# A list scheduler that knows a shared port, bounds that read their own limits, and a new set of rank offsets

## The chip, the cores and the metric

The kernel runs on one core of one Trainium2 chip. The metric is the device time of one execution in microseconds (us). Before the change the median of three runs is 272.78 us (271.49 to 273.32). The core has five engines that matter here, each with its own instruction queue that runs in order: TensorE (PE) multiplies matrices, VectorE (DVE), ScalarE (ACT) and GpSimd (POOL) do elementwise work, and SyncE (SP) issues most of the transfers (DMAs). PE writes into PSUM, a small memory of eight banks from which DVE and ACT read; POOL works on SBUF, the large on-chip memory.

## The reference

Two layers follow each other. The first is attention over 4 batches and 8 heads, 768 positions of 64 numbers, in which each query sees only 6 of the 24 chunks of 32 keys:

```python
k_chunks = k.reshape(B, H, nc, chunk, D)
k_min = np.min(k_chunks, axis=3)
k_max = np.max(k_chunks, axis=3)
ub = np.sum(np.maximum(q[:, :, :, None, :] * k_min[:, :, None, :, :], q[:, :, :, None, :] * k_max[:, :, None, :, :]), axis=-1)
ub = np.where(causal, ub, -1000000000.0)
top_chunks = np.argsort(ub, axis=-1)[..., -top_k:]
scores = scale * np.matmul(q, k.transpose(0, 1, 3, 2))
mask = sel & (pos[:, None] >= pos[None, :])
scores = np.where(mask, scores, -1000000000.0)
...
attn = attn / (np.sum(attn, axis=-1, keepdims=True) + 1e-09)
return np.matmul(attn, v).astype(np.float32)
```

The second is a dense pair of layers over all 3072 tokens: `h = x @ w_in` (512 to 2048), `g = h * clip(h + 3, 0, 6) / 6`, and `g @ w_out` (2048 to 512).

## The kernel before, in words

**Tiling.** Two heads make a pair (16 pairs in all), and 768 queries are two halves of 384, with 12 chunks each. A *unit* is two pairs in one half; there are 16 units, numbered 0 to 15, four to a batch: units 0 and 1 are half 0 of batch 0, units 2 and 3 its half 1, and so on. A dense *group* is one half of one batch: 384 tokens.

**The steps of a unit.** `prepare` turns K and Q so that the head dimension lies on the partitions: in batch 0 by PE (tiles KT and QT, then copies to KF and QF by ACT or DVE), in the other batches by DVE transpositions (L343). Each half of K of a pair then gives 12 chunk limits: the maximum and the minimum of each chunk (`limits`, two DVE reductions, L356 and L357), and their difference (L359, POOL or DVE). The limits are kept in KMA, 32 columns for maximum less minimum and 32 for the minimum, of which 24 are used: columns 0 to 11 for half 0, 12 to 23 for half 1. Q also gives its relu (QR, L367, ACT). Casts by POOL or DVE (L297, L295) put K and Q in bf16 into KL and QLA.

`bounds` (L389) is the matmul that gives the upper bounds UBT of a unit: for each head, the weights are 32 columns of limits (all of a pair's, whichever half the queries are), the moving operand is QF and then QR. For units 4 and later two units are done in one joint step. `attend` then makes, on DVE, the unit's selection: `bounds_in` transposes UBT to UB (and for half 0 adds BIAS, which takes future chunks away), `largest` finds the eight largest (L404), `select` compares with the sixth (L409), writes a shift (L412) into SELA and transposes SELA to the masks MT (L414). Two `masks_out` steps copy MT into QLA beside the queries (L226, L228 or L230: ACT, DVE or POOL). The scores (SPS, L430) then come out of PE with the masks in them; ACT takes the exponentials (PT, L440), POOL clears the triangle (L445), PE multiplies with V (PVP, L461), and DVE divides and writes Xb (L467, L473).

**The dense part of a group.** XT holds the group's tokens turned (by PE and DVE for the first three groups, by DVE transposition and a way through DRAM, BT, BD, BF, for the other five). For each of 16 blocks of the hidden layer PE makes HP (L518), ACT makes U (L523), DVE makes GT (L526); then PE makes three output tiles OP of 16 matmuls each (L533), which ACT or DVE evict to OT (L559, L561) and SP stores.

**What sets the order.** All of this is recorded as steps of a `Plan`, each with the engines that may do it and a length on each, a rank, the steps it comes after, and the buffers that it takes and gives back. `Plan.order` is a list scheduler: it walks through the time of its own model, and whenever an engine is free it starts the ready step of lowest rank for which there are buffers. A step that may go to several engines goes to the one that the model says ends sooner. The rank of a step is its unit's or group's, plus an offset of the kind (the table RANK), plus an offset of the single step from the table SHIFT, whose keys are the numbers of steps in order of their creation; some -2000 is as much as "as soon as possible", +2000 "as late as possible". The kernel's instructions are written out in the order that this gives, each on its engine's queue. On the chip only queues, semaphores and buffers remain: a wait is set wherever an instruction reads or overwrites something that an earlier one in this order wrote or read, by the memory that the two touch.

Four banks of PSUM (`m`) are shared by KT, QT, UBT, PVP, XTP, HP and OP; two double banks (`s`) hold scores. SP's queue has the loads of K, Q and V as well as the stores, in the planner's order, so a load stands behind a store whose tile is not evicted yet.

## Time and profile before

| | |
|---|---|
| median of three runs | 272.78 us |
| profiled execution, its own time | 272.74 us |
| its span, from the first to the last instruction | 271.0 us |
| PE busy | 257.9 us, 95% |
| DVE busy | 220.3 us, 81% |
| ACT busy | 183.1 us, 68% |
| POOL busy | 138.8 us, 51% |
| mean granted clock of PE | 0.994 |

Busy shares are means over stages with different limits. PE's share counts the time in which a matmul is in flight: one that was started and then waits for an input of the next, or runs at a lower clock, counts too. So the profile is read by stage, and within a stage by the spacing of the instructions and by what each of them waited for. In the timeline's rows the first number is the start in us, the second the length; "x16" says that 16 instructions of the kind are merged; and the brackets at the end hold the engine's idle time before the row, and what ended it. The names of instructions are out<-in by tiles. In the rows of groups of instructions the numbers are total busy us, mean ns of one, and the idle time before them.

### The profile page before, as it was taken

Reading aid. Unit: us, or ns where it says so; the run is one execution under the profiler, and the core shown is the slowest. Engines: PE = TensorE matmul, PEld = TensorE weight load, DVE = VectorE, ACT = ScalarE, POOL = GpSimd, SP = SyncE. Lnnn points to the kernel's source line nnn. Section 1 sums busy time; section 2 is a strip of 40 time slices with the busy share of each in tenths; the row PEclk is TensorE's granted clock in tenths of the full one; section 3 lists DMA queues with packets and bytes.
Section 4 is the critical chain, followed back from the end, with each engine's and each line's share of the span. In section 5 each row is a group of like instructions: output and inputs, shape, how many; then the busy total and the mean of one; then the engine's idle time right before and its main releaser. Section 6 shows DMA issues by size and latency. Waiting matters only on the chain.

```text
span 271.0 us, 6300 instructions
## 1 busy us (share of the span) xinstructions
PE 257.9 (95%) x2244; PEld 151.5 (56%) x2244; DVE 220.3 (81%) x605; ACT 183.1 (68%) x297; POOL 138.8 (51%) x309
## 2 busy tenths in 40 slices
...
GB/s 163 221 214 206 203 186 130 182 125 131 194 123 180 146 173 132 158 160 98 137 142 150 190 177 169 54 0 143 93 2 58 60 77 5 95 97 41 39 39 79
DMA packets 122720, 33.70 MB, mean 124 GB/s; under 512 B 113217, under 2 KB 118081, under 8 KB 122689
## 3 DMA queue, kind: packets, MB, share of 16 engines
...
q8 instruction: 17, 0.28, 0.5%
q14 instruction: 15, 0.11, 0.2%
...
## 4 chain that ended last, share of the span: by engine, by line
PE 56%; DVE 27%; ACT 5%; DMA 4%; SPq 3%; issue 2%; ACTq 1%; DVEq 0%
PE OP L533 19%; PE HP L518 19%; PE SPS L430 9%; PE PVP L461 5%; DVE GT L526 4%; PE UBT L389 3%; SPq L210 3%; DVE KMA L357 3%; DVE KMA L356 2%; DMA QS<-in_q_dram 2%; DVE QLA L228 2%; DVE T L404 2%; ACT PT L440 2%; DVE MT L414 2%; DVE Xb L473 2%
## 5 line engine op out<-in xcount | busy, mean ns | idle before, releaser
L440 ACT ACTIVATE PT<-SPS 128x1024 bf16<-128x1024 f32 (+2 forms) x96 | 86.1, 941 | 27.3 <-PE SPS L430 27.0
L518 PE MATMUL HP<-XT,WIN 128*128 128x384 bf16 x512 | 89.4, 326 | 0.2 <-DVE GT L526 0.2
L533 PE MATMUL OP<-WOUT,GT 128*128 128x512 bf16 x368 | 85.5, 379 | 0.0
L523 ACT ACTIVATE U<-HP,THREE 128x384 bf16<-128x384 f32 x128 | 72.6, 611 | 16.7 <-PE HP L518 13.5
L526 DVE SCALAR_TENSOR_TENSOR GT<-U,HP 128x384 bf16<-128x384 bf16 x128 | 66.3, 546 | 16.3 <-ACT U L523 13.3
L518 PEld LDWEIGHTS <-WIN 128*128 128x128 bf16 x512 | 49.3, 98 | 31.0 <-issue 0.3
L445 POOL TENSOR_SCALAR_AFFINE_SELECT PT<-PT 128x256 bf16<-128x256 bf16 x96 | 39.1, 421 | 46.7 <-ACT PT L440 45.5
L533 PEld LDWEIGHTS <-GT 128*128 128x128 bf16 x368 | 35.0, 98 | 37.9 <-issue 1.4
L430 PE MATMUL SPS<-QLA,KL 128*128 128x384 bf16 (+2 forms) x320 | 49.9, 283 | 4.1 <-DVE QLA L228 1.9
L430 PEld LDWEIGHTS <-KL 128*128 128x128 bf16 x320 | 28.4, 99 | 22.4 <-issue 7.4
L297 POOL TENSOR_SCALAR_AFFINE_SELECT KL<-KF 64x384 bf16<-64x384 f32 x63 | 32.0, 508 | 17.2 <-DVE KF L343 12.7
L297 POOL TENSOR_SCALAR_AFFINE_SELECT QLA<-QF 64x384 bf16<-64x384 f32 x60 | 30.6, 510 | 13.5 <-PE SPS L430 6.4
L461 PEld LDWEIGHTS <-PT 128*128 128x128 bf16 x672 | 24.7, 98 | 5.3 <-POOL PT L445 1.1
L461 PE MATMUL PVP<-VB,PT 128*128 128x65 bf16 x672 | 26.2, 194 | 0.3 <-POOL PT L445 0.3
L367 ACT ACTIVATE QR<-QF 128x384 f32<-128x384 f32 x24 | 12.8, 559 | 12.0 <-DVE QF L343 12.0
L473 DVE TENSOR_TENSOR Xb<-PVP,RINV 128x384 bf16<-128x384 f32 x32 | 18.6, 580 | 1.1
L561 DVE TENSOR_SCALAR OT<-OP 128x512 f32<-128x512 f32 x7 | 4.8, 692 | 17.1 <-PE OP L533 17.1
L511 POOL COPY XT<-BF 128x384 bf16<-128x384 bf16 x20 | 9.9, 534 | 15.9 <-DMA BF<-BD 15.9
L559 ACT ACTIVATE OT<-OP 128x512 f32<-128x512 f32 x16 | 9.5, 596 | 12.1 <-PE OP L533 12.0
L356 DVE TENSOR_REDUCE KMA<-KF 128x12 f32<-128x384 f32 x24 | 13.1, 544 | 1.0 <-PE UBT L389 0.6
L228 DVE COPY QLA<-MT 64x768 bf16<-64x768 bf16 x29 | 13.1, 453 | 0.9
L343 DVE STREAM_TRANSPOSE KF<-KS 128x384 f32<-128x384 f32 x24 | 13.2, 561 | 0.0
...
## 6 DMA issues: line engine op xcount, KB each, us to landing
...
KS<-in_k_dram SPq DMA_DIRECT2D x24, 192.0 KB, 5.1
QS<-in_q_dram SPq DMA_DIRECT2D x24, 192.0 KB, 5.9
VT<-in_v_dram SPq DMA_DIRECT2D x24, 192.0 KB, 4.5
...
```

Source lines behind the costliest of these rows:

```text
L228: nc.vector.tensor_copy(to, x)
L297: nc.gpsimd.affine_select(out=to, in_=x, pattern=[[0, n]], compare_op=A.is_ge, fill=0.0, base=0, channel_multiplier=0)
L356: nc.vector.tensor_reduce(out=over, in_=chunks, axis=X_AXIS, op=A.max)
L430: nc.tensor.matmul(SP[:, j, c0:c0 + n], lhsT=KLS[st["pair"] % 6][:, j, jb * P:(jb + 1) * P], rhs=st["QL", half][:, j, at:at + n], start=Tr ...
L440: nc.scalar.activation(PT[:, :, 0:cols], SP[:, :, 0:cols], ACT.Exp, scale=scale)
L445: nc.gpsimd.affine_select(out=PT[:, :, c0:c0 + P], in_=PT[:, :, c0:c0 + P], pattern=[[0, 2], [1, P]], compare_op=A.is_ge, fill=0.0, base=0 ...
L461: nc.tensor.matmul(PVP[:, j, n, :], lhsT=PT[:, j, c0:c0 + P], rhs=st["VB"][:, jb, j, :], start=(jb == 0), stop=(jb == qb))
L473: nc.vector.tensor_tensor(out=to, in0=PVP[:, :, :, 0:D], in1=RINV[:].to_broadcast([P, 2, HB, D]), op=A.mult)
L518: nc.tensor.matmul(HP[:], lhsT=WIN[:, kt, f * P:(f + 1) * P], rhs=g["XT"][:, kt, :, :], start=(kt == 0), stop=(kt == KT_HID - 1))
L523: nc.scalar.activation(U[:], g["HP", f][:], ACT.Relu, bias=THREE[:], scale=1.0)
L526: nc.vector.scalar_tensor_tensor(out=g["GT"][:, f, :], in0=g["U", f][:], scalar=6.0, in1=g["HP", f][:], op0=A.min, op1=A.mult)
L533: nc.tensor.matmul(g["OP", t][:], lhsT=g["GT"][:, f, t * P:(t + 1) * P], rhs=WOUT[:, f, :], start=(f == 0), stop=(f == FT - 1))
```

## The change

The planner gets two things. A step may be marked `port`, and then the model starts a marked DVE step, or any POOL step, only when the other of these two engines is through with such a step; and each PE step has a kind of tiling (`tiles`: "bounds" or none), and the model adds 0.1 us where it changes. Several model lengths change with this.

The selection of a unit becomes up to five steps instead of three: `bounds_in` (the transposition), `future` (BIAS, half 0 only), `largest`, `select`, and `select_out` (the transposition to MT). SELA has two tiles, one for each half, instead of four, and a selection comes after the `select_out` before it of the same half.

The limits lie in KMA in 13 slots of 44 columns, 20 of zeros and then 24 of limits. The bounds of half 1 take the 24 limits and 8 zeros of the slot behind; those of half 0 take 20 zeros and the 12 limits of half 0. The bounds of half 0 are therefore found in columns 20 to 31 of UB.

Because the numbers of steps change, SHIFT is replaced as a whole; RANK stays. By the orders of the two kernels, no engine's total of instructions changes but for these: five mask copies go from DVE to ACT (DVE 29 to 24, ACT 2 to 7), and a few copies and casts change between DVE, ACT and POOL.

```diff
--- before.py
+++ after.py
@@ -25,17 +25,22 @@
 
 
 SHIFT = {
...
-    2046.3, 1409: 34.8, 1412: -200.2, 1460: 182.7, 1466: 73.7, 1494: 165.9, 1500: 13.6, 1527: 53.8, 1557: -171.6
+    55: 1045, 73: 1112.4, 76: 239.7, 77: 132.9, 79: 237.7, 92: 165.4, 93: 130.6, 100: 149.9, 102: 300.3, 108: 7.6, 122: 76.2, 131: -1918.7, 134: -2103.4,
...
+    -1958.8, 1583: -2045.9
 }
 
 
@@ -52,11 +57,11 @@
         self.room, self.steps = {kind: list(range(n)) for kind, n in room.items()}, []
         self.lane, self.lanes, self.lean = 0, room["lane"], {}
 
-    def add(self, engine, length, rank, run=None, after=(), take=(), give=()):
+    def add(self, engine, length, rank, run=None, after=(), take=(), give=(), port=False, tiles=None):
 
 
         step = dict(lengths=engine if isinstance(engine, dict) else {engine: length}, rank=(rank + SHIFT.get(len(self.steps), 0), len(self.steps)),
-                    run=run, told=isinstance(engine, dict), take=take, give=give, then=[])
+                    run=run, told=isinstance(engine, dict), port=port, tiles=tiles, take=take, give=give, then=[])
         step["wait"] = {e: len(after) for e in step["lengths"]}
         for other in after:
             other["then"].append(step)
@@ -86,6 +91,7 @@
     def order(self, **busy):
 
         free = {e: busy.get(e, 0.0) for e in self.BEHIND}
+        port, tiles = dict(DVE=0.0, POOL=0.0), None
         ready = {e: [] for e in self.BEHIND}
 
         def behind(step, own):
@@ -125,8 +131,15 @@
                         for held in st["take"]:
                             held[2] = self.take(held[0])
                         out.append(st)
-                        st["at"], st["engine"], st["length"] = now, e, st["lengths"][e]
-                        free[e] = now + st["length"]
+                        begin = now
+                        if e == "POOL" or e == "DVE" and st["port"]:
+                            begin = max(now, port["DVE" if e == "POOL" else "POOL"])
+                            port[e] = begin + st["lengths"][e]
+                        if e == "PE":
+                            begin += 0.1 * (st["tiles"] != tiles)
+                            tiles = st["tiles"]
+                        st["at"], st["engine"], st["length"] = begin, e, st["lengths"][e]
+                        free[e] = begin + st["length"]
                         n += 2
                         heapq.heappush(events, (free[e], n, st, True))
                         heapq.heappush(events, (free[e] + self.BEHIND[e], n + 1, st, False))
@@ -165,6 +178,8 @@
     HS = S // 2
     HC = NCH // 2
     scale = 1.0 / np.sqrt(D)
+    OWN = 32 - HC
+    KM = NCH + OWN
 
     const = ctx.enter_context(tc.tile_pool(name="const", bufs=1))
     ps_score = ctx.enter_context(tc.tile_pool(name="ps_score", bufs=1, space=bass.MemoryType.PSUM))
@@ -257,12 +272,12 @@
     nc.gpsimd.memset(BIAS[:], 0.0)
     nc.gpsimd.affine_select(out=BIAS[:], in_=BIAS[:], pattern=[[1, 8], [-1, 8]], compare_op=A.is_ge,
                             fill=-1e9, base=0, channel_multiplier=0)
-    SELA = const.tile([P, 4, HC, 32], BF16, name="SELA")
+    SELA = const.tile([P, 2, HC, 32], BF16, name="SELA")
     nc.gpsimd.memset(SELA[:], 0.0)
     THREE = const.tile([P, 1], FP32, name="THREE")
     nc.vector.memset(THREE[:], 3.0)
-    KMA = const.tile([P, 6, 2, 32], FP32, name="KMA")
-    nc.vector.memset(KMA[:, :, :, HC:32], 0.0)
+    KMA = const.tile([P, 13, KM], FP32, name="KMA")
+    nc.vector.memset(KMA[:, :, 0:KM - NCH], 0.0)
     for r in (0, 96):
         nc.vector.tensor_scalar(EB[r:r + 32, :].rearrange("p (c w) -> p c w", w=CH),
                                 IDENT32[r:r + 32, r:r + NCH].unsqueeze(2).to_broadcast([32, NCH, CH]), -MASK,
@@ -308,8 +323,7 @@
     for i in range(6):
         KLS.append(const.tile([P, 2, S], BF16, name=f"KL{i}"))
     QLS = [QLA[:, i, :, :] for i in range(6)]
-    KMS = [KMA[:, i, :, :] for i in range(6)]
-    SELS = [SELA[:, i, :, :] for i in range(4)]
+    SELS = [SELA[:, i, :, :] for i in range(2)]
     VBS = [const.tile([P, NBLK, 2, D + 1], BF16, name=f"VB{i}") for i in range(6)]
 
     xpool = ctx.enter_context(tc.tile_pool(name="xpool", bufs=1))
@@ -351,7 +365,7 @@
     def limits(st, half, part, e="DVE"):
 
         chunks = st["KS", half][:].rearrange("p (c w) -> p c w", w=CH)
-        over, low = (KMS[st["pair"] % 6][:, which, half * HC:(half + 1) * HC] for which in range(2))
+        over, low = (KMA[:, 2 * (st["pair"] % 6) + which, KM - NCH + half * HC:KM - NCH + (half + 1) * HC] for which in range(2))
         if part == 0:
             nc.vector.tensor_reduce(out=over, in_=chunks, axis=X_AXIS, op=A.max)
             nc.vector.tensor_reduce(out=low, in_=chunks, axis=X_AXIS, op=A.min)
@@ -375,6 +389,11 @@
     def at_column(u, i, j):
 
         return 2 * (j if u["n"] % 2 and u["joint"] else 1 - j) + i
+
+    def chunk_limits(st, half, which):
+
+        c0 = (2 * (st["pair"] % 6) + which) * KM + (KM - NCH) * half
+        return KMA[:].rearrange("p s c -> p (s c)")[:, c0:c0 + 32]
 
     def bounds(us):
         for u in us:
@@ -386,30 +405,35 @@
                     for j in range(2):
                         r = slice(64 * j, 64 * j + 64)
                         g = 32 * at_column(u, i, j)
-                        nc.tensor.matmul(u["UBT"][g:g + 32, :], lhsT=KMS[st["pair"] % 6][r, which, :],
+                        nc.tensor.matmul(u["UBT"][g:g + 32, :], lhsT=chunk_limits(st, u["half"], which)[r, :],
                                          rhs=(st["QR", u["half"]] if which == 0 else st["QS", u["half"], "F"])[r, :], start=(which == 1), stop=(which == 0))
 
     def bounds_in(u):
         UB = u["UB"] = work.tile([P, HC, 32], FP32, name="UB", tag=tag("ub"), bufs=1)
         nc.vector.transpose(UB[:].rearrange("p t c -> p (t c)"), u["UBT"][:])
-        if u["half"] == 0:
-            nc.vector.tensor_tensor(out=UB[:, 0:8, 0:8], in0=UB[:, 0:8, 0:8], in1=BIAS[:], op=A.add)
+
+    def future(u):
+        nc.vector.tensor_tensor(out=u["UB"][:, 0:8, OWN:OWN + 8], in0=u["UB"][:, 0:8, OWN:OWN + 8], in1=BIAS[:], op=A.add)
 
     def largest(u):
         T8, UB, half = small.tile([P, HC, 8], FP32, name="T8", tag="t8"), u["UB"], u["half"]
         u["T8"] = T8
         if half == 0:
-            nc.vector.tensor_reduce(out=T8[:, 0:TOPK, 0], in_=UB[:, 0:TOPK, 0:TOPK], axis=X_AXIS, op=A.max)
+            nc.vector.tensor_reduce(out=T8[:, 0:TOPK, 0], in_=UB[:, 0:TOPK, OWN:OWN + TOPK], axis=X_AXIS, op=A.max)
         for t in range(0 if half else TOPK, HC):
-            nc.vector.max(out=T8[:, t, :], in_=UB[:, t, 0:max(8, half * HC + t + 1)])
+            c0 = 0 if half else OWN
+            nc.vector.max(out=T8[:, t, :], in_=UB[:, t, c0:c0 + max(8, half * HC + t + 1)])
 
     def select(u):
-        SEL, T8, UB, half = SELS[u["n"] % 4], u["T8"], u["UB"], u["half"]
-        at, nch = (slice(0, HC), NCH) if half else (slice(TOPK, HC), HC)
+        SEL, T8, UB, half = SELS[u["half"]], u["T8"], u["UB"], u["half"]
+        at, nch, c0 = (slice(0, HC), NCH, 0) if half else (slice(TOPK, HC), HC, OWN)
         nc.vector.scalar_tensor_tensor(
             out=SEL[:, at, 0:nch], in0=T8[:, at, TOPK - 1:TOPK].to_broadcast([P, at.stop - at.start, nch]), scalar=-5e8,
-            in1=UB[:, at, 0:nch], op0=A.max, op1=A.is_gt)
+            in1=UB[:, at, c0:c0 + nch], op0=A.max, op1=A.is_gt)
         nc.vector.tensor_scalar(SEL[:, :, NCH:NCH + 1], T8[:, :, 0:1], CAP, 0.0, op0=A.subtract, op1=A.max)
+
+    def select_out(u):
+        SEL, half = SELS[u["half"]], u["half"]
         MT = u["MT"] = work.tile([P, HS], BF16, name="MT", tag=tag("mt"), bufs=1)
         nc.vector.transpose(MT[:], SEL[:].rearrange("p t c -> p (t c)"))
 
@@ -650,7 +674,7 @@
     vs = hold("gt", 2 * H // 2, 1)
     for i in range(6):
         late = there["WOUT", 0] if i >= 4 else []
-        made["EB", i] = [add(dict(POOL=0.85) if late else dict(DVE=0.52, ACT=0.81), None, 25 if late else RANK["eb"], later(beside, i, j), after=late)
+        made["EB", i] = [add(dict(POOL=0.85) if late else dict(DVE=0.52, ACT=0.81), None, 25 if late else RANK["eb"], later(beside, i, j), port=True, after=late)
                          for j in range(2)]
         made["ones", i] = add("POOL", 0.17, 25 if late else -3, later(ones, i), after=late)
     n_queries = 0
@@ -694,11 +718,11 @@
                                        after=here + (in_order[-1:] if name == "QS" else []), take=[held[f]], give=used)
 
             a = turned["KS"]
-            made["K", p, half] = [add(castings(first), None, r + lead + 1, later(keys, st, half, j),
+            made["K", p, half] = [add(castings(first), None, r + lead + 1, later(keys, st, half, j), port=True,
                                       after=[a] + free.get(("KL", p - 6), []), give=[held["kf"]]) for j in range(2)]
             b1 = add("DVE", 0.95 if first else 0.93, r + lead, later(limits, st, half, 0), after=(direct["KS"] if first else [a]) + free.get(("KM", p - 6), []),
                      give=[bank_of["KS"] if first else held["kf"]])
-            chain.append(add(dict(POOL=0.17, DVE=0.08) if first else dict(POOL=0.17), None, r + lead, later(limits, st, half, 1), after=[b1]))
+            chain.append(add(dict(POOL=0.17, DVE=0.08) if first else dict(POOL=0.17), None, r + lead, later(limits, st, half, 1), after=[b1], port=True))
 
             st["QL", half] = QLS[n_queries % 6]
             n_queries += 1
@@ -709,7 +733,7 @@
                 u["qf", p][1] = 4
             chain += [c, add(dict(ACT=0.45, DVE=0.5) if first else dict(ACT=0.42), None, r + lead, later(queries, st, half, "relu"), after=direct["QS"] if first else [c],
                              take=[u["qr", p]], give=[bank_of["QS"] if first else u["qf", p]])]
-            made["Q", p, half] = [add(castings(first), None, r + lead + 1, later(queries, st, half, j),
+            made["Q", p, half] = [add(castings(first), None, r + lead + 1, later(queries, st, half, j), port=True,
                                       after=[c] + free.get(("QL", n_queries - 7), []), give=[u["qf", p]]) for j in range(2)]
             st["q", half] = n_queries - 1
 
@@ -718,14 +742,14 @@
             r = 10.0 * us[0]["n"]
             used = [u[name, st["pair"]] for u in us for st in u["two"] for name in ("qf", "qr")]
             held = [hold("m") for u in us]
-            a = add("PE", 1.5 * slow if len(us) == 1 else 1.9, r + RANK["sel"], later(bounds, us), after=sum([u["chain"] for u in us], []),
+            a = add("PE", 1.36 * slow if len(us) == 1 else 1.38, r + RANK["sel"], later(bounds, us), tiles="bounds", after=sum([u["chain"] for u in us], []),
                     take=held, give=used)
             for u, m in zip(us, held):
                 u["bounds"], u["ubt"] = a, m
                 for st in u["two"]:
                     free.setdefault(("KM", st["pair"]), []).append(a)
 
-    held_results = {}
+    held_results, selected = {}, {}
 
     def attend(u):
         nonlocal order_of_scores
@@ -733,12 +757,16 @@
         n, two, half = u["n"], u["two"], u["half"]
         r = 10.0 * n
         ub, mt = hold("ub"), hold("mt", 2)
-        a = add("DVE", 0.94 if half == 0 else 0.61, r + RANK["sel"], later(bounds_in, u), after=[u["bounds"]], take=[ub], give=[u["ubt"]])
-        a = add("DVE", 0.59 if half == 0 else 1.07, r + RANK["sel"], later(largest, u), after=[a])
-        a = add("DVE", 1.07 if half == 0 else 1.25, r + RANK["sel"], later(select, u), after=[a], take=[mt], give=[ub])
+        a = add("DVE", 0.51, r + RANK["sel"], later(bounds_in, u), after=[u["bounds"]], take=[ub], give=[u["ubt"]])
+        if half == 0:
+            a = add("DVE", 0.17, r + RANK["sel"], later(future, u), after=[a], port=True)
+        a = add("DVE", 0.56 if half == 0 else 1.0, r + RANK["sel"], later(largest, u), after=[a])
+        a = add("DVE", 0.29 if half == 0 else 0.52, r + RANK["sel"], later(select, u), after=[a] + selected.get(half, []), give=[ub], port=True)
+        a = add("DVE", 0.55, r + RANK["sel"], later(select_out, u), after=[a], take=[mt])
+        selected[half] = [a]
         mask = []
         for j in range(2):
-            mask.append(add(dict(DVE=0.46, ACT=0.83, POOL=0.9), None, r + RANK["sel"] + j, later(masks_out, u, j),
+            mask.append(add(dict(DVE=0.46, ACT=0.83, POOL=0.9), None, r + RANK["sel"] + j, later(masks_out, u, j), port=True,
                             after=[a] + mask + sum([free.get(("QL", st["q", half] - 6), []) for st in two], []), give=[mt]))
 
         begun = []
@@ -765,7 +793,7 @@
                     if q0 == jb * P:
                         parts.append(add("POOL", 0.37, r + RANK["tri"], later(triangle, st, half, t, c0), after=[e]))
             if st["b"] == 0:
-                parts.append(add(dict(ACT=0.42, DVE=0.35), None, r - 3, later(cast_values, st, half), after=there["V", p, half], give=[vs]))
+                parts.append(add(dict(ACT=0.42, DVE=0.46), None, r - 3, later(cast_values, st, half), after=there["V", p, half], give=[vs], port=True))
                 parts.append(made["ones", p])
                 if half == 1:
                     parts.append(made["V", p])
```

24 rows, old and new, of the table SHIFT are left out of this document.

## The prediction

> **What bounds the kernel now.** First the page's busy shares, then stages cut where TensorE (PE) changes its rate.
>
> ```profile
> PE 257.9 (95%) x2244; PEld 151.5 (56%) x2244; DVE 220.3 (81%) x605; ACT 183.1 (68%) x297; POOL 138.8 (51%) x309
> ```
>
> ```profile
> 0.00:3.75 3.75, 0.00 (x0) 0.03 (x1) 2.75 (x5) 0.79 (x1) 3.00 (x13) 1.00 0.52 116
> 3.75:29.61 25.86, 20.95 (x156) 11.50 (x157) 23.97 (x77) 19.87 (x37) 21.08 (x50) 1.00 1.22 214
> 29.61:36.97 7.36, 7.22 (x65) 4.32 (x65) 6.00 (x15) 4.66 (x6) 3.72 (x9) 0.77 1.18 201
> 36.97:267.40 230.43, 229.72 (x2025) 135.61 (x2023) 186.83 (x509) 157.74 (x255) 111.00 (x242) 1.00 0.66 113
> 267.40:271.00 3.60, 0.00 (x0) 0.00 (x0) 0.76 (x2) 0.00 (x0) 0.00 (x0) 1.00 0.23 75
> ```
>
> Each row gives the length, then busy time of PE, its weight loads, VectorE (DVE), ACT and POOL, then the granted clock. From 36.97 us, where the first dense matmul (HP) stands, PE is busy 229.72 of 230.43 us. Its work is the same in both kernels, so a new order can win only the time that PE spends badly. That lies in two places. Until 29.61 us DVE is busy 23.97 of 25.86 us and PE merely follows it. Later, a few instructions last too long because they hold an input that is not ready. The last 3.60 us (eviction and store) stay as they are.
>
> The second place shows in the timeline, at the joint bounds (UBT) of two units: a clean group first, then two others.
>
> ```profile
> 85.16 1.45 PE UBT L389 x32
> ...
> 76.75 1.50 PE L389 MATMUL UBT<-QF,KMA 64*32 64x384 f32 x12
> 77.04 0.54 DVE L357 TENSOR_REDUCE KMA<-KF 128x12 f32<-128x384 f32 x1
> 77.69 0.15 PEld L389 LDWEIGHTS UBT<-QF,KMA 64*32 64x32 f32 x5 [0.79 <-ACT QR L367]
> 79.15 5.35 PE L533 MATMUL OP<-WOUT,GT 128*128 128x512 bf16 x24
> ...
> 120.86 1.34 PE L389 MATMUL UBT<-QF,KMA 64*32 64x384 f32 x14
> 121.09 0.54 DVE L357 TENSOR_REDUCE KMA<-KF 128x12 f32<-128x384 f32 x1
> 121.69 0.11 PEld L389 LDWEIGHTS UBT<-QF,KMA 64*32 64x32 f32 x2 [0.66 <-DVE KMA L357]
> 123.10 1.25 PE L533 MATMUL OP<-WOUT,GT 128*128 128x512 bf16 x5
> ```
>
> The clean group holds PE for 1.45 us. The one at 76.75 holds it until the next OP at 79.15, 2.40 us; the one at 120.86 until 123.10, 2.24 us. In both a weight load waits in the middle and goes on about 0.1 us after a reduction of L357 has ended (77.04 + 0.54, and 121.09 + 0.54). By the order of steps those reductions make limits of the *second* half (pairs 6 and 11), while the bounds are those of the first. The matmuls wait for numbers that they multiply only into columns nobody reads, because their weights are all 32 columns of a pair's limits. The row at 77.69 names ACT, which I take to be a coincidence of semaphores.
>
> **The change, part by part.** *Half's bounds read their own limits.* The half-0 weights become 20 zeros and 12 own limits, so the wait above has no object. Gain: 2.40 - 1.45 = 0.95 us and 2.24 - 1.45 = 0.79 us, together **1.74 us**. Lower end: 0, if Q or its relu comes just as late. In the new order the last Q transposition that the first group needs is the 169th DVE instruction where it was the 180th; for the second it is the 302nd where it was the 308th, while PE comes to them within 1 us of its work as before. So Q should not be late next, and I take the whole.
>
> *Selection in five steps, two SELA tiles, BIAS at columns 20 to 27.* Counts and shapes are those of before. A selection now waits for the transposition of the preceding one on the same half, but both are on DVE, which runs in order: 0. SELA's memset halves and KMA's grows by a twelfth, in the first 4 us.
>
> ```profile
> 3.75 1.91 PE L334 MATMUL KT<-IDENT,KS 128*128 128x128 f32 x6 [3.75 <-DMA KS<-in_k_dram]
> ```
>
> SELA's memset is one of POOL's tasks in its 3.00 busy us of the first stage; shortening it could let PE start sooner only if K did not land last, and by the row it does. I take 0, at best some tenths.
>
> *The order in the first 37 us.* DVE sets it, so I count what stands on DVE ahead of the masks of unit 2, whose scores begin PE's unbroken run at 29.61.
>
> ```profile
> 5.62 0.56 DVE L356 TENSOR_REDUCE KMA<-KT 128x12 f32<-128x384 f32 x1 [1.13 <-ACT KF L226]
> 6.10 0.55 DVE L357 TENSOR_REDUCE KMA<-KT 128x12 f32<-128x384 f32 x1
> 6.56 0.55 DVE L228 COPY KF<-KT 128x384 f32<-128x384 f32 x1
> ...
> L228 DVE COPY QLA<-MT 64x768 bf16<-64x768 bf16 x6 | 3.1, 518 | 0.2
> L473 DVE TENSOR_TENSOR Xb<-PVP,RINV 128x384 bf16<-128x384 f32 x2 | 1.1, 558 | 0.1
> L228 DVE COPY QF<-QT 128x384 f32<-128x384 f32 x2 | 1.1, 548 | 0.0
> L228 DVE COPY KL<-EB 64x768 bf16<-64x768 bf16 x2 | 1.0, 521 | 0.1
> ```
>
> The new order has there four reductions more at their spacing of 0.47 (6.10 to 6.56), +1.9; one KF copy more, +0.5; two QF copies fewer, -1.1; two mask copies fewer, -1.0 (ACT makes them); one eviction Xb fewer, -0.6; and two KL copies moved into the idle 1.13 us ahead of 5.62 with one put in outside, net -0.5. Sum: **-0.8**; unit 2's scores come so much sooner.
>
> ```profile
> 34.88 0.56 DVE L486 COPY XT<-XTP 128x768 bf16<-128x768 bf16 x1 [0.28 <-PE XTP L482]
> 36.33 0.58 DVE L394 STREAM_TRANSPOSE UB<-UBT 128x384 f32<-128x384 f32 x1 [0.90 <-PE UBT L389]
> 38.85 0.58 DVE L414 STREAM_TRANSPOSE MT<-SELA 128x384 bf16<-128x384 bf16 x1
> ```
>
> Ahead of the last XT copy the four reductions cancel, and unit 3's bounds and selection, 36.33 to 38.85 or 2.5 us, come in front. Against that stand the savings above but for the eviction, 2.1, and the 0.28 idle: XT stays at 35.44, 1.5 us before HP starts at 36.97. So PE can begin HP 0.8 us sooner and does not yet wait for XT.
>
> *The port.* The planner now delays a marked DVE step while it has POOL at work, and the reverse.
>
> ```profile
> 16.89 0.87 DVE L228 COPY QLA<-MT 64x768 bf16<-64x768 bf16 x2
> 22.81 1.50 DVE L228 COPY QLA<-MT 64x768 bf16<-64x768 bf16 x2
> 97.89 0.36 DVE L228 COPY QLA<-MT 64x768 bf16<-64x768 bf16 x1
> ```
>
> Two mask copies take 0.87 or 1.50 us, and one alone can take 0.36. Against that the startup's six, of 518 ns in the mean, lose 6 x 0.16 = 1.0 us. POOL has the same number of steps in both orders, so I let 0.2 us of this go and keep 1.0 either way for the range. The startup gives **-1.0**, from -2.0 to 0.
>
> [...]
>
> *Tiling.* The planner pays 0.1 us when PE changes to or from UBT. Ten groups of bounds stand in either order, so nothing goes. *The rest after 37 us*: five mask copies move from DVE to ACT (five fewer of 29, two of them in the startup), in slack ACT has; I count 0. PE's idle time there is 0.7 us in all (229.72 of 230.43).
>
> **Sum.** The profiled execution took 272.74 us, 1.7 more than its span, and stands at the median of 272.78. 272.74 - 1.0 - 1.74 = **270.0 us**.
>
> **Rivals.** *The loads come late (slower side).*
>
> ```profile
> 80.67 3.17 SPq L565 DMA_DIRECT2D out_dram<-OT  x2
> 83.94 3.63 SPq L210 DMA_DIRECT2D KS<-in_k_dram  x4
> 87.68 5.22 SPq L210 DMA_DIRECT2D QS<-in_q_dram  x4
> KS<-in_k_dram SPq DMA_DIRECT2D x24, 192.0 KB, 5.1
> QS<-in_q_dram SPq DMA_DIRECT2D x24, 192.0 KB, 5.9
> 84.50 0.66 PE SPS L430 x6
> 98.53 0.91 PE PVP L461 x30
> 98.28 0.58 DVE L343 STREAM_TRANSPOSE KF<-KS 128x384 f32<-128x384 f32 x1
> 102.98 1.03 DVE L343 STREAM_TRANSPOSE QF<-QS 128x384 f32<-128x384 f32 x2
> 100.00:120.00 20.00, 20.00 (x202) 13.18 (x201) 19.80 (x45) 17.76 (x30) 15.54 (x36) 1.00 1.07 146
> ```
>
> The K and Q of units 8 and 9 are issued at 83.94 and 87.68, behind two stores. In the new order the last quarter of that K and all of that Q stand behind one more store, whose output tile PE ends later: by 16 OP matmuls (16 x 0.22 = 3.5), 16 score matmuls (16 x 0.11 = 1.8), 12 PVP (12 x 0.03 = 0.4) and a joint UBT (1.45), 7.1 us. Before, the last K lands near 83.94 + 3.63 + 5.1 = 92.7 and is used at 98.28, 5.6 us of slack; Q near 92.9 + 5.9 = 98.8, used at 102.98, 4.2 us. So K would come 1.5 us late and Q 2.9 us. The transpositions stand in DVE's queue; behind them wait reductions, GT and Xb, and PE waits for those. DVE is busy 19.80 of 20 us there and cannot win it back. For it: the slack is smaller than the move. Against it: PE has dense fill at that place. Up to 4.4 us reach PE if both waits do: 270.0 + 4.4 = **274.4**, slower than before. It decides from the point where the late store costs over 2.7 us; with K's part alone, 271.5.
>
> *The clock dip falls elsewhere.*
>
> ```profile
> 29.00:30.00 1.00, 0.34 (x1) 0.11 (x2) 0.95 (x4) 0.00 (x0) 1.00 (x3) 0.99 1.12 204
> ```
>
> In the third stage the granted clock is 0.77, a loss of 0.23 x 7.36 = 1.7 us with PE fully loaded; just ahead of it PE was busy 0.34 of 1 us. The new order fills this stretch otherwise: without the dip **268.3**, with a second one 271.7. [...]
>
> *The change does not do what it says.* If the two groups waited for Q's relu on ACT, as the row at 77.69 names, and the offsets only shuffle the startup, the time stays **272.7**.
>
> **How the numbers follow.** Forecast 270.0, both gains within 1 us: 0.42. The same with the port's 1.0 gained too, 269.0: 0.10. No dip, 268.3: 0.16; a second dip, 271.7: 0.04. Late loads, 271.5 to 274.4: 0.15. No gain, 272.7: 0.05. A stall where I did not look in a long order, above 274.4: 0.08. The range leaves out this last one and a little at the other end, where no dip and the port's gain come together: 267.2 to 274.2. About 1% (270.05 to 275.5) is what a measurement of this kernel can tell from no change. Faster by over 1% are half of the forecast's cases, the port's and those without a dip: 0.21 + 0.10 + 0.16 = 0.47. Slower by over 1% is the unseen stall with the worst of the late loads, 0.10. Within 1%: 0.43.
>
> **What would show it.** Joint bounds groups all near 1.45 us, with no weight load waiting for L371, the reductions' new line; the first HP near 36 us; PE busy in the rest in all but a few tenths, with a rest shorter than 230.43 by 1.7. Wrong would make it: DVE idle for a KF or QF with a DMA as its releaser near 90 to 104 us; HP still at 37 us; a group above 2 us again; a clock below 0.77 in the stage from 30 us.

## The result, and the profile after

The changed kernel takes 274.01 us (median of 18 runs, 273.07 to 279.39) where the kernel before takes 272.54 (271.49 to 273.32): 1.0058 times the time, 95% interval 1.0041 to 1.0074. A second set of its runs (e15_again below) gives 274.04 us and 1.0058 (1.0038 to 1.0078). The forecast was 270.0. Here and below a ratio rests on the runs within 1.5% of the fastest of the same kernel, a median and a range on all of them.

The profiled execution is the fastest of its 18, 273.07 us. So I read the profile of e15_again, an ordinary run, beside it where the two differ. First the page's span and busy shares, then the stages cut as in the prediction (length, busy time of PE, weight loads, DVE, ACT, POOL, the granted clock; the last two figures are DMA): the first two fences are the profile after, the third is e15_again.

```profile
span 271.4 us, 6309 instructions
...
PE 255.6 (94%) x2244; PEld 151.0 (56%) x2244; DVE 216.9 (80%) x600; ACT 185.8 (68%) x302; POOL 137.1 (51%) x309
```

```profile
3.75:30.46 26.71, 19.67 (x144) 10.85 (x143) 23.95 (x76) 20.44 (x39) 20.63 (x47) 0.96 1.26 215
30.46:37.73 7.27, 6.74 (x77) 4.20 (x77) 5.89 (x26) 5.40 (x7) 3.28 (x8) 0.93 1.19 198
37.73:267.23 229.50, 228.92 (x2025) 135.63 (x2023) 183.56 (x492) 159.14 (x258) 110.82 (x242) 1.00 0.61 112
267.23:271.40 4.17, 0.00 (x0) 0.00 (x0) 0.76 (x2) 0.00 (x0) 0.00 (x0) 0.89 0.19 65
```

```profile
30.44:38.22 7.78, 7.25 (x76) 4.59 (x76) 5.86 (x26) 5.39 (x7) 3.62 (x9) 0.86 1.19 198
38.22:267.86 229.64, 227.87 (x2006) 135.66 (x2023) 182.84 (x492) 158.95 (x258) 110.76 (x242) 1.00 0.65 112
267.86:272.00 4.14, 0.00 (x1) 0.00 (x0) 0.76 (x2) 0.00 (x0) 0.00 (x0) 0.95 0.19 65
```

Before, the first HP stood at 36.97, the rest took 230.43 and the end 3.60 us. So three terms make the difference. The first HP is 0.76 us later (1.25 in e15_again), the rest 0.9 shorter (0.8), the end 0.5 longer: +0.4 and +1.0, the growth of the spans from 271.0 to 271.4 and 272.0. The medians differ by 1.5: the profiled execution before was 0.2 slower than its median, those two were 0.9 and 0.4 faster than theirs.

The startup, in PE's timeline of the profile after (start, length, line, tile, count; in brackets the wait before it and what ended it):

```profile
25.35 0.32 PE L454 MATMUL SPS<-QLA,KL 128*128 128x384 bf16 x1
28.66 1.12 PE L454 MATMUL SPS<-QLA,KL 128*128 128x384 bf16 x5 [2.98 <-POOL QLA L312]
29.57 0.86 PE L485 MATMUL PVP<-VB,PT 128*128 128x65 bf16 x12
30.46 1.54 PE L454 MATMUL SPS<-QLA,KL 128*128 128x384 bf16 x8
...
37.73 0.81 PE L542 MATMUL HP<-XT,WIN 128*128 128x384 bf16 x4
```

PE waits 2.98 us in one piece for a cast by POOL, the second cast of pair 3's first-half queries. Its place on POOL's queue is the following (timeline of POOL, same kernel), behind triangles and the casts of later units; before, it was one of six casts done near 15.5 us. Only after it come pair 3's scores and a set of values, and then unit 2's scores at 30.46, 0.85 later than before.

```profile
25.88 0.51 POOL L312 TENSOR_SCALAR_AFFINE_SELECT QLA<-QF 64x384 bf16<-64x384 f32 x1
26.46 1.04 POOL L469 TENSOR_SCALAR_AFFINE_SELECT PT<-PT 128x256 bf16<-128x256 bf16 x2
27.47 0.21 POOL L373 TENSOR_TENSOR KMA<-KMA 128x12 f32<-128x12 f32 x1
27.64 0.40 POOL L469 TENSOR_SCALAR_AFFINE_SELECT PT<-PT 128x256 bf16<-128x256 bf16 x1
28.10 0.51 POOL L312 TENSOR_SCALAR_AFFINE_SELECT QLA<-QF 64x384 bf16<-64x384 f32 x1
```

DVE, which was to have unit 2's masks 0.8 us sooner, waits on its way there (timeline of DVE, profile after, then before, then e17_lastbest, whose steps are the same up to this place):

```profile
11.79 0.58 DVE L413 STREAM_TRANSPOSE UB<-UBT 128x384 f32<-128x384 f32 x1 [0.28 <-PE UBT L408]
13.12 0.56 DVE L383 TENSOR_SCALAR QR<-QT 128x384 f32<-128x384 f32 x1 [0.42 <-ACT QF L241]
```

```profile
12.68 0.58 DVE L394 STREAM_TRANSPOSE UB<-UBT 128x384 f32<-128x384 f32 x1
```

```profile
11.21 0.57 DVE L413 STREAM_TRANSPOSE UB<-UBT 128x384 f32<-128x384 f32 x1
```

The new order brings DVE to unit 0's bounds at 11.2 to 11.6 us, and PE may not be through with them. A matmul of these bounds takes 0.84 us until the trace's record of the clock begins, at full speed, and 0.48 us from then on; the 1.00 that the stage rows show for the first microseconds is no measured clock. In the 17 traces of the new order the record begins at 10.05 to 13.71 us. Where it does by 10.23 (e1, e5, e17), DVE does not wait for these bounds, and the last step of unit 2's selection ends at 27.32 to 27.50; in the other 14, from 10.95 on, DVE waits 0.16 to 0.80 us, and that step ends at 28.16 to 28.98. In the old order it ends at 28.39 to 28.52, and DVE never waits there.

The joint bounds (PE's timeline, profile after): the first group is clean, with 1.45 us from 76.52 to the next matmul at 77.97; the other, before at 120.86 with 2.24, now at 120.30, still takes 1.87, and 2.32 in e15_again.

```profile
76.52 0.88 PE L408 MATMUL UBT<-QF,KMA 64*32 64x384 f32 x16
77.18 0.85 PE L408 MATMUL UBT<-QR,KMA 64*32 64x384 f32 x16
77.97 0.82 PE L542 MATMUL HP<-XT,WIN 128*128 128x384 bf16 x4
...
120.30 0.97 PE L408 MATMUL UBT<-QF,KMA 64*32 64x384 f32 x12
122.17 1.04 PE L557 MATMUL OP<-WOUT,GT 128*128 128x512 bf16 x4
```

What holds this group now is a late load of Q (timelines of DVE and of the weight loads, profile after):

```profile
118.40 1.04 DVE L357 STREAM_TRANSPOSE QF<-QS 128x384 f32<-128x384 f32 x2 [0.94 <-DMA QS<-in_q_dram]
120.01 0.59 DVE L497 TENSOR_TENSOR Xb<-PVP,RINV 128x384 bf16<-128x384 f32 x1
120.72 0.15 PEld L408 LDWEIGHTS UBT<-QF,KMA 64*32 64x32 f32 x5 [0.26 <-issue]
```

DVE waits for the load, so Xb behind it is late, and the group's second half goes on 0.1 us after Xb has ended (in e15_again too). Xb reads a PVP, and PVP and UBT share four banks; that the group waits for this bank is not shown, since the profile names no releaser. The link with the load is: over the 17 traces of the new order the group takes 1.45 to 1.68 us where DVE waits for this Q 0.66 us or less, and 1.87 to 2.48 where it waits 0.82 to 1.44.

Last, the waits (engine, line, waited for: total, times, longest). The first two rows are DVE's in the profile after, from 88 to 136 us: the loads of K and Q for units 8 and 9. The second pair are SP's last waits, the first row before, the second after: the end waits 1.0 us instead of 0.5 at most for the last stores.

```profile
DVE QF L357 <- DMA QS<-in_q_dram: 0.9, 1, 0.9
...
DVE KF L357 <- DMA KS<-in_k_dram: 0.2, 1, 0.2
```

```profile
SPq L889 <- DMA out_dram<-OT: 0.7, 2, 0.5
```

```profile
SPq L917 <- DMA out_dram<-OT: 1.2, 2, 1.0
```

### The profile page after: what moved, and what is told of

Its sections match the earlier page's. It is cut to its first block, busy times and chain, and to the rows that moved or that the text cites. A ratio compares the mean times of both kernels' runs of the same rounds, so it can differ in the third digit from the quotient of the medians.

```text
span 271.4 us, 6309 instructions
## 1 busy us (share of the span) xinstructions
PE 255.6 (94%) x2244; PEld 151.0 (56%) x2244; DVE 216.9 (80%) x600; ACT 185.8 (68%) x302; POOL 137.1 (51%) x309
## 4 chain that ended last, share of the span: by engine, by line
PE 71%; DVE 12%; DMA 7%; POOL 3%; ACT 2%; issue 2%; SPq 1%; ACTq 0%; DVEq 0%; POOLq 0%
PE HP L542 26%; PE OP L557 24%; PE SPS L454 9%; PE PVP L485 6%; DMA KS<-in_k_dram 5%; PE UBT L408 4%; DMA QS<-in_q_dram 2%; ACT PT L464 2%; DVE GT L550 2%; POOL PT L469 1%; PE OP L565 1%; SPq L225 1%; DVE QF L357 1%; DVE KF L357 1%; DVE KMA L370 1%
## 5 line engine op out<-in xcount | busy, mean ns | idle before, releaser
L464 ACT ACTIVATE PT<-SPS 128x1024 bf16<-128x1024 f32 (+2 forms) x96 | 85.9, 935 | 12.9 <-PE SPS L454 11.2
L542 PE MATMUL HP<-XT,WIN 128*128 128x384 bf16 x512 | 91.0, 326 | 0.2 <-DVE GT L550 0.2
L547 ACT ACTIVATE U<-HP,THREE 128x384 bf16<-128x384 f32 x128 | 71.2, 603 | 15.6 <-PE HP L542 13.1
L312 POOL TENSOR_SCALAR_AFFINE_SELECT KL<-KF 64x384 bf16<-64x384 f32 x61 | 30.8, 507 | 18.0 <-DVE KF L357 12.9
L312 POOL TENSOR_SCALAR_AFFINE_SELECT QLA<-QF 64x384 bf16<-64x384 f32 x62 | 31.4, 507 | 10.6 <-PE SPS L454 3.9
L357 DVE STREAM_TRANSPOSE QF<-QS 128x384 f32<-128x384 f32 x24 | 12.7, 557 | 1.0 <-DMA QS<-in_q_dram 0.9
```

The source lines that it names most:

```text
L312: nc.gpsimd.affine_select(out=to, in_=x, pattern=[[0, n]], compare_op=A.is_ge, fill=0.0, base=0, channel_multiplier=0)
L357: nc.vector.transpose(T[:], st[name][:, st["i"], half * HC:(half + 1) * HC, :].rearrange("p c e -> p (c e)"))
L464: nc.scalar.activation(PT[:, :, 0:cols], SP[:, :, 0:cols], ACT.Exp, scale=scale)
L542: nc.tensor.matmul(HP[:], lhsT=WIN[:, kt, f * P:(f + 1) * P], rhs=g["XT"][:, kt, :, :], start=(kt == 0), stop=(kt == KT_HID - 1))
L547: nc.scalar.activation(U[:], g["HP", f][:], ACT.Relu, bias=THREE[:], scale=1.0)
```

## The experiments

All start from the kernel after, unless the kernel before is named; "behind(n, m)" takes step n out of the written-out list and puts it right after step m. The diffs are shortened to what differs, those of e1_cast and e4_loads are written in this form, and the remarks behind # are for the reader.

```
    steps = plan.order(PE=3.7, ACT=3.8, DVE=4.2, POOL=3.2, SP=3.7, DMA=1.6)
    number = {step["rank"][1]: step for step in steps}

    def behind(n, other):
        steps.remove(number[n])
        steps.insert(steps.index(number[other]) + 1, number[n])
```

This table is drawn from the traces of all of them. "MT" is the end of the transposition MT that closes unit 2's selection (DVE, L438, before L414), "S" the start of unit 2's scores, "HP" the first HP, "rest" from there to PE's end. The ratio is that to the kernel before in the same session. A row's times are of one execution, and not always a typical one: after and e1_cast were profiled in the shortest of their runs, e3_shared, e5_warm and e11_wout in the longest, e6_castwarm at 279.28 us, while its ratio rests on its four runs of 273.84 to 275.51.

| run | MT | S | HP | S to HP | rest | ratio (95%) |
|---|---|---|---|---|---|---|
| before | 28.51 | 29.61 | 36.97 | 7.36 | 230.40 | 1 |
| after | 28.16 | 30.46 | 37.73 | 7.27 | 229.50 | 1.0058 (1.0041 to 1.0074) |
| e15_again | 28.39 | 30.44 | 38.22 | 7.78 | 229.64 | 1.0058 (1.0038 to 1.0078) |
| e1_cast | 27.41 | 29.37 | 38.27 | 8.90 | 229.92 | 1.0111 (1.0088 to 1.0134) |
| e2_own (on before) | 28.39 | 29.50 | 36.85 | 7.35 | 229.23 | 0.9974 (0.9960 to 0.9988) |
| e3_shared | 28.98 | 31.27 | 39.36 | 8.09 | 230.82 | 1.0112 (1.0093 to 1.0131) |
| e4_loads | 28.66 | 30.71 | 38.58 | 7.87 | 228.57 | 1.0028 (1.0014 to 1.0042) |
| e5_warm | 27.50 | 31.14 | 37.95 | 6.81 | 234.89 | 1.0138 (1.0108 to 1.0169) |
| e6_castwarm | 28.29 | 30.25 | 37.05 | 6.80 | 235.96 | 1.0092 (1.0065 to 1.0118) |
| e7_startup | 28.49 | 29.40 | 38.96 | 9.56 | 229.89 | 1.0062 (1.0042 to 1.0082) |
| e8_all | 28.36 | 29.27 | 38.85 | 9.58 | 228.74 | 1.0021 (1.0003 to 1.0038) |
| e9_castwarmwout | 28.85 | 30.81 | 37.61 | 6.80 | 230.92 | 1.0092 (1.0072 to 1.0112) |
| e10_warmwout | 28.34 | 31.98 | 40.32 | 8.34 | 230.83 | 1.0167 (1.0139 to 1.0195) |
| e11_wout | 28.28 | 30.58 | 39.33 | 8.75 | 230.05 | 1.0087 (1.0057 to 1.0116) |
| e12_best | 28.91 | 31.00 | 37.75 | 6.75 | 228.09 | 0.9990 (0.9979 to 1.0001) |
| e13_bankwarm | 28.48 | 30.53 | 37.33 | 6.80 | 237.65 | 1.0313 (1.0290 to 1.0335) |
| e14_bankbest | 28.48 | 29.40 | 36.15 | 6.75 | 230.08 | 0.9990 (0.9957 to 1.0022) |
| e16_latecast (on before) | 28.52 | 30.76 | 37.63 | 6.87 | 230.09 | 1.0022 (1.0009 to 1.0035) |
| e17_lastbest | 27.32 | 28.24 | 34.99 | 6.75 | 229.57 | 0.9943 (0.9927 to 0.9959) |
| e18_warmwout | 28.64 | 30.68 | 37.49 | 6.81 | 230.52 | 1.0081 (1.0057 to 1.0105) |

Up to the first HP, after, e15_again, e4_loads and e11_wout are the same program, and their HP stands at 37.73 to 39.33. So a difference of some tenths in HP between two rows is no effect by itself. The time from MT to S is steadier (2.05 to 2.30 in these four), and so is that from S to HP once the windows of halved clock in it are counted (the clock, below).

### One part each: the cast, the limits, the loads

**e1_cast**

```diff
-    for step in plan.order(...):
+    behind(138, 137)
+    for step in steps:
```

> After the change, with one step moved in the written-out order: GpSimd's second cast of pair 3's first-half queries (QLA<-QF at 28.10) goes right behind its sister, from 52nd to 28th on GpSimd's queue; every other step keeps its place. Theory (the position of this cast on GpSimd's queue, not the number of its steps, is what the startup lost): the 2.98 us wait of PE at 25.68 goes, the first HP comes at 35.0 to 36.2 instead of 37.73, and the time falls by 1.5 to 2.5 us against the changed kernel, to about 272. Rival (VectorE's masks or ScalarE's copies bound the first 37 us anyway, and the wait only moves): the first HP stays above 37.2 and the time falls by 0.5 us at most.

The wait for POOL is gone and unit 2's scores come 1.1 us sooner than in the profile after, yet the first HP stands at 38.27 and the time is 1.0111. The theory in this simple form falls. Most of the 1.1 us is not the cast's either: MT ends 0.75 us sooner in this execution, and from MT to the scores it takes 1.96 us instead of 2.30 (2.05 in e15_again). PE's waits in e1_cast from 23 to 31 us show what is next, and the same view of ACT why:

```profile
PE SPS L454 <- ACT PT L464: 3.5, 1, 3.5
```

```profile
ACT QLA L241 <- DVE MT L438: 2.4, 1, 2.4
```

ACT's queue has unit 2's mask copy ahead of pair 3's two exponentials; it waits for DVE's MT, and the ready exponentials wait behind it. Before, both mask copies were DVE's.

**e2_own** (kernel before, own limits alone)

```diff
-    KMA = const.tile([P, 6, 2, 32], FP32, name="KMA")
+    KMA = const.tile([P, 13, KM], FP32, name="KMA")
...
-                        lhsT=KMS[st["pair"] % 6][r, which, :],
+                        lhsT=chunk_limits(st, u["half"], which)[r, :],
```

> The kernel before, its order of steps unchanged, with the bounds of each half reading only its own limits (the new layout of KMA and the column shift OWN in what reads UB; SELA as two tiles by half to make the space). Theory (false dependence: the joint groups at 76.75 and 120.86 waited in the middle for reductions of limits that they do not use): both groups take 1.45 us instead of 2.40 and 2.24, and the time falls by 1.7 us against the kernel before, to about 270.9. Rival (these groups wait for the relu of the queries or for something else in the order that ends as late): the groups stay above 2 us or the time comes back in the next wait, and the gain is 0 to 0.4 us.

271.52 us against 272.39. Neither group waits for limits any more; the first, in PE's timeline, and the place where part of the gain goes again:

```profile
76.64 0.88 PE L395 MATMUL UBT<-QF,KMA 64*32 64x384 f32 x16
77.31 0.85 PE L395 MATMUL UBT<-QR,KMA 64*32 64x384 f32 x16
78.09 5.35 PE L540 MATMUL OP<-WOUT,GT 128*128 128x512 bf16 x23
...
108.27 0.81 PE L525 MATMUL HP<-XT,WIN 128*128 128x384 bf16 x4 [0.39 <-DVE GT L533]
```

The false wait was real and took 1.45 instead of 2.40 us once its object was gone. The rest shrinks by 1.17 us, not 1.74: the second group holds PE for 1.68 us, 0.23 more than the first, and PE, now ahead, meets DVE at 108 us, where nobody waited before. The time falls by 0.7 us (0.3 to 1.1).

**e3_shared** (limits of before in the new order)

```diff
-        c0 = (2 * (st["pair"] % 6) + which) * KM + (KM - NCH) * half
-        return KMA[:].rearrange("p s c -> p (s c)")[:, c0:c0 + 32]
+        return KMA[:, st["pair"] % 6, which, :]
```

> The kernel after, its order of steps unchanged, with the shared limits of before (KMA 6x2x32, bounds of a first half read all 24 limits, OWN = 0). If the own limits carry the 1.7 us in the new order too, this is 1.7 us slower than the changed kernel, with two or more joint groups above 2 us. If the new order has the second half's reductions behind the first-half bounds only where these do not wait, it is 0 to 0.3 us slower, and the 1.7 us was already a matter of the order.

275.49 us, half a per cent above the changed kernel, but no joint group waits: those at 78.14, 87.03 and 123.33 all have rows of 0.88 and 0.85 us. In the new order the reductions no longer stand ahead of those groups but behind them, and the false wait changes sides: DVE must not overwrite limits that the bounds still read (DVE's timeline).

```profile
79.76 0.55 DVE L369 TENSOR_REDUCE KMA<-KF 128x12 f32<-128x384 f32 x1 [1.59 <-PE UBT L406]
...
124.99 0.55 DVE L369 TENSOR_REDUCE KMA<-KF 128x12 f32<-128x384 f32 x1 [0.93 <-PE UBT L406]
```

Neither profile of the changed kernel has such a wait; the kernel before has one of 0.61 us, at 122.73. The rest is 1.2 us longer than in e15_again. MT is 0.6 us later too and the first HP 1.1, but executions of one startup differ by as much.

**e4_loads**

```diff
+    for n in range(448, 462, 2):
+        behind(n, n - 2)
```

> The kernel after, with the loads of K parts 2 to 4 and Q parts 1 to 4 of units 8 and 9 moved on SP ahead of the two output stores that stand before them, right behind K's first part. Theory (late loads cost time between 90 and 140 us): VectorE's waits for the QF and KF loads (0.9 and 0.2 us) go and the time falls by 0.5 to 1.2 us against the changed kernel. Rival (the loads are late but VectorE has slack there, or the stores pushed back hold an output buffer): 0, at most 0.2 us either way.

273.41 us; 1.0028 against 1.0058 is 0.8 us less. DVE's two waits for these loads are gone and the rest is 228.57, 1.0 us shorter than in both profiles of the changed kernel, and 1.83 shorter than before. The late loads were a loss of their own, and without them the second joint group takes 1.68 us and the rest gains what own limits promised.

### The clock

**e7_startup** and **e8_all**

```diff
+    behind(138, 137)      # the cast, as in e1_cast
+    behind(260, 189)      # ACT: unit 2's mask copy behind pair 3's exponentials
+    behind(261, 259)      # DVE: the other mask copy right behind MT's transposition
+    for n in range(448, 462, 2):      # e8_all only: the loads, as in e4_loads
+        behind(n, n - 2)
```

> The kernel after with three steps moved in the written-out order: the cast as in e1_cast; ScalarE's copy of unit 2's first mask behind the two exponentials of pair 3 that stood behind it; VectorE's copy of the second mask right behind the transpose of MT. Theory (two in-order queues held the start, GpSimd's by the cast and ScalarE's by a mask copy that waits for VectorE with ready exponentials behind it): unit 2's scores start at 28.0 to 28.5 instead of 30.46, the first HP comes at 35.5 to 36.5, and the time falls by 1.5 to 2.5 us against the changed kernel, to 271.5 to 272.5. Rival (VectorE's chain to unit 2's masks, or a later wait, ends as late anyway): 0.5 us at most.

> e7_startup and the earlier loads of e4_loads together. If the two losses are separate they add up: 0.6 us less than e7_startup, 270.9 to 271.9, which would be under both kernels. If the earlier start only runs into the loads (they are not moved by an earlier HP), it is the same as e7_startup.

274.07 and 273.01 us. The loads again give their part (0.4%), but three queue places put right gain nothing at HP: unit 2's scores start at 29.40, as early as before, and HP follows 9.56 us later instead of 7.36. The stage rows (columns as above; the seventh figure is the granted clock) of e7_startup:

```profile
25.00:28.00 3.00, 1.50 (x28) 1.26 (x29) 2.93 (x18) 2.34 (x4) 2.86 (x8) 1.00 1.16 222
28.00:31.00 3.00, 1.60 (x8) 0.91 (x8) 2.90 (x9) 1.38 (x2) 2.87 (x8) 0.61 1.14 209
31.00:34.00 3.00, 3.00 (x31) 1.35 (x28) 1.07 (x4) 1.39 (x2) 1.82 (x5) 0.50 1.15 201
34.00:37.00 3.00, 2.79 (x31) 1.78 (x27) 2.10 (x14) 1.06 (x2) 0.18 (x1) 0.76 1.22 198
```

PE idles 1.5 us of 3, and then runs at half clock through the stretch in which it is the bound. 3 x (0.39 + 0.50 + 0.24) = 3.4 us of full clock are missing, which is 6.8 us at one half: two windows of 3.4. The trace's own record of the clock says the same: one half from 28.63 to 35.46. It has one window before (from 29.98), after (28.13) and in e15_again (29.21), so the place differs between executions of one kernel too. In the records of before and after 17.07 us at full speed, 3.41 at one half and 238.93 at full speed follow each other, 5, 1 and 70 times 3.41. In e7_startup PE was never idle for more than 2.54 us at a time (its wait ahead of 29.40) and did 1.50 us of work in the 3 us from 25.00, so the clock fell behind a stretch that was idle only in part.

**e5_warm, e6_castwarm, e9_castwarmwout, e10_warmwout** keep PE busy through its wait, by matmuls whose result nobody reads.

```diff
+    def warm(st):
+        for _ in range(27):
+            nc.tensor.matmul(st["SP", 0, 1][:, 0, 256:512], lhsT=KLS[st["pair"]][:, 0, 0:P],
+                             rhs=st["QL", 0][:, 0, 0:256], start=True, stop=True)
+    # e5, e10: behind step 155, pair 2; e6, e9: with behind(138, 137), behind step 165, pair 3
+    behind(73, 92)        # e9, e10 only: POOL's issue of WOUT's second megabyte
```

> The kernel after with 27 extra matmuls of 256 columns (about 2.9 us) on PE in the place where it waits for the late cast (behind the values of pair 0 in unit 0); they write columns of a score bank that nothing reads, so the result is the same. They take nothing off any wait: they only keep PE busy ahead of the stretch from 28.7 us. Theory (the long idle stretch brings on the halved clock just where PE is the bound, unit 2's scores to the first HP): the granted clock is 1.0, the first HP comes at 36.7 to 37.2, and the time falls by 0.7 to 1.5 us against the changed kernel, with a narrower spread. Rival (the engines that feed PE bound that stretch too, the halved clock is hidden): 0 to 0.4 us, which is what the runs of the kernel before without a halved clock show against those with one (272.04 against 272.46).

> The same 27 extra matmuls in the run with the earlier cast (e1_cast), placed where that one now waits (behind the values of pair 1 in unit 0). If e1_cast lost its gain to a second window of halved clock, this is 1.5 to 2.2 us faster than e1_cast, with unit 2's scores at 29.4 as there and the first HP near 36 to 36.5, and 0.5 us faster than e5_warm. If the wait for ScalarE (mask copy ahead of the exponentials) is all that holds e1_cast, it is the same as e1_cast within 0.4 us.

> e6_castwarm with one more step moved: GpSimd's issue of the second megabyte of WOUT goes behind its two copies for pair 5 (from 42.1 us to about 44.2 there), so that the fourth K load of units 4 and 5, issued at 42.1, is 2 us ahead of it as in the kernel before. Theory (that load shared the DMA engines with WOUT and landed 5 us late, which is the 4.6 us wait of PE at 50.9 to 55.4 in e6_castwarm; under it, keeping the clock up gains what a window of halved clock costs): no wait on VectorE for KF at 47 to 53 us, first HP near 37, and 271.8 to 272.8 us, 2.6 to 3.6 less than e1_cast. Rival (the late K load has another cause, or the extra matmuls cost elsewhere): the wait stays, above 274.

> e5_warm with the same later issue of WOUT: the kernel after, with PE kept busy through its 3 us wait. This gives the price of the halved clock alone in the changed kernel. Theory: 0.5 to 1.4 us less than the changed kernel (272.6 to 273.5), first HP 37.2 to 38.0. Rival (clock hidden): 273.6 to 274.2.

276.68, 275.37, 274.74 and 277.09 us: as times, all misses. But up to the first HP the clock is whole in e5, e6 and e9, and there HP follows unit 2's scores by 6.80 us. Two side effects spoil the times, and e9 meets the late loads of units 8 and 9: DVE waits 1.2 us for K at 114 us, and PE 0.9 us for DVE at 117. In e5 and e10 the extra matmuls write columns that the exponential does not read, and yet it waits for them; ACT's waits in e10_warmwout, 24 to 31 us:

```profile
ACT PT L464 <- PE SPS L899: 3.5, 1, 3.5
```

That made the cast later still, and in e10 the halved clock came back behind the idle piece of 1.63 us that was left (e5 has the same piece and no halved window). The other side effect, in e5 and e6, is a collision of loads, next.

**e13_bankwarm** and **e18_warmwout** write to a free bank instead, so no exponential waits.

```diff
+        W = ps_mix.tile([P, 512], FP32, name="WARM", tag="m1")
+        for _ in range(18):
+            nc.tensor.matmul(W[:, 0:384], lhsT=KLS[st["pair"]][:, 0, 0:P], rhs=st["QL", 0][:, 0, :], start=True, stop=True)
+    # behind step 155, pair 2
+    behind(73, 92)        # e18 only
```

> The kernel after with 18 extra matmuls of 384 columns (2.9 us) in PE's wait for the late cast, this time into a free bank of the second PSUM pool that no other engine reads, so that no exponential waits for them (in e5_warm and e10_warmwout ScalarE waited 3.2 and 3.5 us for the extra matmuls, and the cast came 0.9 to 1.8 us later). This is the price of the halved clock alone. Theory (PE is the bound from 28.7 us to the first HP, so a window of halved clock there costs 0.5 us and a second one 2 more): first HP 8.8 to 9.2 us after the end of unit 2's MT transpose instead of 9.57, 0.5 to 1.5 us faster than the changed kernel in the same session. Rival (hidden): within 0.3 us of it.

> e13_bankwarm (the changed kernel with PE kept busy through its wait by 18 extra matmuls in a free bank) with WOUT's issue behind the two copies for pair 5, which takes away the collision that made e13_bankwarm 281 us. The price of the halved clock alone: first HP at 37.3 as there (38.22 in e15_again), no wait for KF near 48 us, and 272.7 to 273.4 us, 0.7 to 1.3 less than the changed kernel's 274.0. Rival (what the clock gives is taken by the loads): 273.7 or more with a wait on KF, QF or GT between 45 and 120 us.

First HP 8.85 us after MT in both, where the changed kernel has 9.57 and 9.83: one window of halved clock costs it 0.7 to 1.0 us up to there (e11_wout, with two, has 11.05). The times are 280.99 and 274.52 us. In e18 the gain is spent again behind it: the rest is 230.52, 0.9 longer than in e15_again. DVE waits 0.7 us for K at 113 us, and PE 0.7 us for DVE at 115; the later WOUT may add to it (e11_wout has a rest of 230.05). So the price of the first window does not reach the end in the changed kernel while the loads are late. That of a second one can: of the changed kernel's runs, the 13 with one window have a median of 273.74 us and the three others that are not near 279 take 274.84 to 275.80. In e15_again the two runs with two windows, 273.60 and 274.59 us, are no longer than the rest.

### The loads at 42 us

**e11_wout**

```diff
+    behind(73, 92)
```

> The kernel after with only the issue of WOUT's second megabyte moved behind the two copies for pair 5. If the 1.4 us by which the changed kernel's fourth K load is ahead of WOUT is enough, nothing changes in the ordinary run: 273.6 to 274.2. If WOUT delays that load already, 0.3 to 1 us is gained, and the runs near 279 that the changed kernel has now and then do not appear.

274.80 us: no gain. Its first HP is at 39.33, after two windows of halved clock, and the rest is half a microsecond longer. It serves as the control for the pair above and below. None of its six runs is near 279 us, where two of the 18 of the changed kernel are; none of e15_again's six is either, so this decides nothing.

Why e13 loses 8.6 us, and the profiled executions of e5 (278.75) and e6 (279.28) some 6, is seen in e13_bankwarm: DVE's waits from 44 to 58 us, PE's timeline, and the K loads' time to landing (shortest, median, longest) from 38 to 58 us.

```profile
DVE KF L357 <- issue: 5.6, 1, 5.6
```

```profile
55.21 5.19 PE L542 MATMUL HP<-XT,WIN 128*128 128x384 bf16 x16 [4.08 <-DVE GT L550]
```

```profile
DMA to landing us min/median/max: 4.6/5.5/10.6
```

The fourth K load of units 4 and 5 goes out on SP's queue at 41.2 to 43.4 us in every kernel, whatever PE does; WOUT's second megabyte is issued by POOL behind triangles, so it moves forward with PE. Where WOUT follows that load by 0.0 (e6), 0.05 (e13) or 0.29 us (e5), the load lands after 10.3 to 11.0 us and DVE waits 5 to 6 us for K; where it follows by 1.0 us (e9) or more (2.22 before, 1.42 after, 2.07 e15_again), it lands after 4.1 to 5.7 us. The changed kernel has less of this room than the kernel before, and asks for this K 3.4 us sooner (first KF at 47.75, before at 51.17).

### The late cast alone, and all losses out

**e16_latecast** (kernel before; POOL's order alone changes)

```diff
+    for n, other in ((138, 234), (180, 138), (181, 180), (184, 181), (185, 184)):
+        behind(n, other)
```

> The kernel before with one step moved the other way: GpSimd's second cast of pair 3's first-half queries goes from the six casts near 15.5 us to behind the cast of pair 2's keys at 28.4 us, where the new order has it; all else in its order. If the late cast is what the startup lost (PE waits for it in one piece, and 1.8 us of scores and values are left to do when unit 2's masks are there), PE waits 2 to 3 us before pair 3's scores, unit 2's scores start 0.5 to 1 us later than 29.61, often with two windows of halved clock, and the time is 0.6 to 2 us above the kernel before. If unit 2's masks (30.03) are the bound: within 0.3 us of it.

273.03 us against 272.39, 0.6 us (0.2 to 1.0). PE's timeline:

```profile
28.95 1.12 PE L430 MATMUL SPS<-QLA,KL 128*128 128x384 bf16 x5 [2.72 <-POOL QLA L297]
...
30.76 1.75 PE L430 MATMUL SPS<-QLA,KL 128*128 128x384 bf16 x8
...
37.63 1.46 PE L518 MATMUL HP<-XT,WIN 128*128 128x384 bf16 x8
```

The same wait appears in the kernel before. MT ends where it did, and unit 2's scores follow it by 2.24 us instead of 1.10, as in the changed kernel (2.30 and 2.05): up to the scores the cast's place is the whole loss. HP comes 0.66 us later, at the low end of what was expected, because the stretch behind the scores takes 6.87 us here instead of 7.36: 1.5 us of the window of halved clock lie in it, and all 3.4 in the profile before.

**e12_best, e14_bankbest, e17_lastbest** put everything together: the three queue places, the loads, WOUT's issue, and PE kept busy.

```diff
+    behind(138, 137); behind(260, 189); behind(261, 259)
+    for n in range(448, 462, 2):
+        behind(n, n - 2)
+    behind(73, 92)        # e17: behind(73, 332)
+    # e12: 20 extra matmuls in a score bank; e14, e17: 15 in the free bank; behind step 165
```

> e8_all (cast, mask copies, loads) with 20 extra matmuls (2.2 us) in PE's remaining wait at 26.7 us and the later issue of WOUT. If clock, queues and loads are separate terms that add up: unit 2's scores at 29.3 as in e8_all, first HP 6.8 us later at 36.1 (there 9.6 later, at 38.85), the rest 228.7 as there, so 270.0 to 271.0 us, below both kernels. If something else takes the place of the halved clock: 272 or more.

> e12_best with its extra matmuls (15 of 384 columns) in the free bank too, so that the exponential of pair 3 no longer waits 1.74 us for them and ScalarE's mask copy no longer 1 us after that. Theory: unit 2's scores at 29.3 to 29.6 instead of 31.00, the first HP near 36.3 instead of 37.75, and 270.4 to 271.0 us against the 271.87 of e12_best. If it stays above 271.5 the first HP is held by something else.

> e14_bankbest with the issue of WOUT's second megabyte one triangle later on GpSimd's queue (behind the triangle of pair 2 that follows the copies for pair 5), so that it stands 2 us or more behind the fourth K load of units 4 and 5 instead of 1.13. Theory (the runs of e14_bankbest from 273 to 280 are those in which WOUT overtakes that load; there is no wait when it is 1.0 us or more behind, and a wait of 5 us at 0.3 or less): the first HP stays near 36.2, all runs lie within 270.3 to 271.8, below both kernels. Rival (the loads up to 70 us are simply too late for so early a start): spread and median as in e14_bankbest.

e12_best takes 271.87 us; its extra matmuls hold an exponential, and with it the mask copy. e14_bankbest has HP at 36.15, but WOUT only 1.13 us behind the K load: its twelve runs go from 270.69 to 280.3 with a median of 277.10, and the ratio 0.9990 rests on five of them. In the profiled one of 272.96 us the load is in time but for 0.2 us; that WOUT overtakes it in the seven long ones is argued, none of them was profiled. In e17_lastbest WOUT is 2.28 us behind, all runs lie between 270.67 and 271.47, and the ratio is 0.9943 (0.9927 to 0.9959): 1.5 us under the kernel before and 3.1 under the changed one. K lands after 5.6 us, and DVE, which asks for it sooner here, still waits 1.4 us, to 0.2 us behind the landing. The granted clock is whole, and HP stands at 34.99. That is 1.2 us before e14's only because MT ended at 27.32 in this execution; from MT to HP both take 7.67 us, where the kernel before takes 8.46.

```profile
26.79 1.46 PE L905 MATMUL WARM<-QLA,KL 128*128 128x384 bf16 x8
28.24 1.03 PE L454 MATMUL SPS<-QLA,KL 128*128 128x384 bf16 x8
...
34.99 0.81 PE L542 MATMUL HP<-XT,WIN 128*128 128x384 bf16 x4
```

**e15_again**

```diff
 (no edit: the kernel after)
```

> The kernel after, unchanged, beside the others of this call on the same chip: 273.4 to 274.5 us. It says what part of the differences between calls is the chip's.

274.04 us, as foretold. Its figures stand in the table.

## Why the prediction was wrong

**Own limits, -1.74: right in mechanism, too large.** The wait was false, as e2_own shows. Two steps failed. "So Q should not be late next" went by Q's place on DVE's queue and not by the landing of its load: in the changed kernel this load is late, and the second group takes 1.87 and 2.32 us where it took 2.24 (1.68 in e4_loads, with the loads moved). The lower end named just this, and the rival on loads named the load; the two were not put together. "I take the whole" failed as well: in e2_own, where Q is in time, 1.17 us arrive at PE's end and 0.7 in the time, because PE meets DVE's GT at 108 us. The prediction looked for the next late thing only at the groups themselves, not behind them. The new order alone would not have done it: with shared limits the false wait is DVE's there, 1.59 and 0.93 us (e3_shared).

**The order in the first 37 us, -0.8: wrong, +0.8 to +1.25.** Two steps failed. First, "PE merely follows it", by which DVE's own instructions gave the time and its waits were put at nothing. MT ends 0.1 to 0.35 us sooner (28.16 and 28.39 for 28.51), not 0.8, because DVE comes to unit 0's bounds before PE has them and then waits for ACT too, 0.7 and 1.2 us together. The count itself holds: in the three traces with hardly a wait there MT ends 1.0 to 1.2 us sooner. Second, and this decides the sign, the step "POOL has the same number of steps in both orders", by which POOL and its queue were taken as no bound. The number says nothing; one cast that stood beside its sister now stands 25 places behind it. It puts 1.14 us between MT and unit 2's scores, and 0.66 us on HP, by itself (e16_latecast). It leaves PE idle in one piece of 3 us, and then with more to do after the masks. Behind it stands the next queue: ACT's mask copy in front of ready exponentials still keeps the scores 1.96 us behind MT (e1_cast), and with both put right it is 0.91 (e7_startup).

**The clock.** The rivals had the dip gone (0.16) or doubled (0.04), at 1.7 us each way. An accident it is in part, but the order sets the odds. A window takes 3.4 x 0.5 / 271 = 0.006 off a run's mean granted clock. By that, 29 of 93 runs of the kernel before in five sessions have no window and the others one, while of the 24 runs of the changed kernel none is without and seven have two or more. The price was too large: the runs before without a window have a median of 271.88 us, those with one 272.46 and 272.59 (0.994 and 0.991), so 0.6 to 0.7 us. The changed kernel pays 0.7 to 1.0 us at the first HP (e13_bankwarm, e18_warmwout). The clock also hid the cure: e7_startup wins 1.1 to 1.4 us between MT and unit 2's scores and loses it to a second window.

**The port, -0.2.** The four mask copies that DVE still makes in the startup have a mean of 0.50 us, against 0.52 before: no gain can be seen. That POOL's work made the copies of 0.87 and 1.50 us long was assumed; no run shows it, and none shows POOL's side. The rival with the port's gain should have had 269.2 and not 269.0: 0.2 of the 1.0 us was in the forecast already.

**Tiling and the rest after 37 us, 0: wrong by the loads.** The rival "the loads come late" was right in kind: DVE waits for Q and K at the place named, 0.9 and 0.2 us (2.9 and 1.5 in its sum), and e4_loads prices the loss at 1.0 us of the rest and 0.8 of the time, below the 1.5 to 4.4 worked out. Of that, 0.2 to 0.6 us is the second joint group (1.87 and 2.32 us against 1.68). "Decides from 2.7 us" was for that rival alone; together with the startup it took less.

**"The last 3.60 us stay as they are": wrong by 0.5.** In every kernel with the new order the end is 4.1 us or longer, in those with the old one 3.6; the last store is issued 0.4 us after its eviction instead of 0.1, and the slowest of the last two lands 2.0 us after its issue (after, e15_again, e17_lastbest) instead of 1.8. Why was not tried and stays open.

The sum, then, by e15_again: +1.25 at the first HP, -0.76 in the rest, +0.5 at the end.
